# Local dilated attention gated by a SiLU feed-forward: the feed-forward of groups 2 and 3 by threes, one more attention chunk turned by DMA through spent key tiles

## The chip, the cores and the metric

One core of a Trainium2 chip runs the whole kernel. The metric is the device time of one execution in microseconds (us). Before the change it is 624.95 us, the median of three runs from 624.53 to 624.99 us.

## What is computed

The input is x with 2048 positions of 640 features, in float32. A layer norm of x feeds two branches, whose product is added to x:

```python
xn = _layernorm(x, axis=-1)
s = _A_ref(xn, A_wqkv, A_wo)          # attention, then a projection with wo
g = _silu(_B_ref(xn, B_w1, B_w2))     # silu(silu(xn @ w1) @ w2)
return x + s * g
```

The attention has 32 heads of 20 features. Each position looks at eight positions: its own and those 2, 4, ... 14 before it. w1 is 640 x 1536 and w2 is 1536 x 640.

## The kernel before, in words

**Tiles and groups.** The 2048 positions are cut into four groups of 512; the code counts them g = 0 to 3, and this text calls them group 1 to 4, as the change's title does. A group is a half of the sequence and a parity of its positions, so that the dilation of 2 becomes a dilation of 1 inside a group. In a group each of the 128 partitions holds T = 4 neighbouring positions. The 640 features are DC = 5 chunks of 128.

**Exact products out of rounded ones.** TensorE multiplies in the type float32r. To keep accuracy, every factor is split into a rounded high half and the rest (`th` and `tl` for data, `wh` and `wl` for weights, `sh` and `sl` inside the feed-forward), and each product is three matmuls: high by high, low by high, high by low.

**The stages.** For each group `qkv_phase` makes queries, keys and values in four quarters of 160 columns (`NQ = 4`), each quarter with 5 chunks x 4 tiles of positions x 3 matmuls into four of the six accumulator banks `acc`. ScalarE empties the banks (`evac_qkv`) into the tiles `Q[q]` and `KV[q]`. `KV[q]` holds K and V of one quarter with HALO = 7 earlier positions ahead of them; these come from the neighbour partition, so `halo` shifts 127 rows by one partition and 126 rows by two with DMAs. VectorE then does the attention of that quarter (`scores`, `values`) into the tile `O`. This runs long behind TensorE: VectorE finishes a group's attention while TensorE is in that group's feed-forward and the next group's quarters.

`ffn_phase` runs the feed-forward: `up(f)` makes one of FC = 12 chunks of the hidden layer (15 matmuls of 512 columns into a bank `rot`, then two SiLUs on ScalarE and a subtraction on VectorE), and `down(f)` multiplies that chunk by w2 into six `acc` banks. Within it lies `wo_phase`, the projection of the *previous* group's attention. For that, the previous group's `O` has to be turned (features on the partitions), chunk by chunk. There are two ways: `o_chunk` turns a chunk on TensorE (`split_t`, line 636: four transposes), and `turn_o` turns it by DMA (ScalarE copies the chunk into one tile, two DMA transposes carry it into a second tile, ScalarE joins it, VectorE makes the low half). The table `ON_DMA` says for each group which chunks go by DMA, and when.

**Weights.** 100 and more weight tiles pass through a ring of RING = 7 tiles `w0` to `w6`. At its first uses a weight is loaded raw (line 538) and split on the fly by ScalarE (line 573) and VectorE (line 577); at one of these uses the two halves are stored in DRAM (line 581, tiles `half_...`), and later uses load both halves at once with a DMA from the GpSimd queue (line 564), 640 KB each for a feed-forward chunk. A ring tile is loaded again when TensorE is done with it, and, where its halves are being stored, when that store has landed. The weights of the projection, wo, are split a second time and stored in group 3: `half_wo_0` to `half_wo_4`.

**What sets the order.** TensorE's order is the order in which the code records its operations (`plan(g)` for the feed-forward). All other engines get theirs from a list scheduler, `Weave`, that works with estimated durations and priorities; it orders the SP queue and the GpSimd queue too. An engine and a queue then run their list strictly in that order. In `halo`, each shift is cut at row 112, so it is issued as a DMA of 112 rows and one of 15 or 14 rows (line 751).

**What the steps of the prediction touch.** PE is TensorE, DVE is VectorE, ACT is ScalarE, POOL is GpSimd, SP is the queue that issues most DMAs. Line 636 is a transpose on TensorE, 751 a halo DMA, 581 a store of weight halves, 564 a load of them, 1130 to 1132 the matmuls of `up`, 1003 and 1005 those of `down` and of the projection, 956 to 958 those of the quarters, 1048 to 1051 the residual rows of a group (load, add on POOL, store).

Of the kernel before, what the change touches and what calls it, by code (L numbers as in the profile page):

```python
# [15 lines left out]
P = 128  # L16
S, D, F, H, DH = 2048, 640, 1536, 32, 20
# [4 lines left out]
CQ = HQ * DH  # L22
# [7 lines left out]
CA, CB = 384, 256  # L30
RING = 7
NS = 3
SINGLE = 6
RAW_AHEAD = 10
TURNS = 1
FIRST_AT = 44.0, 60.0
# [6 lines left out]
SUB_LATE = 3  # L43
ADD_LATE = 3
X_BY = {1: 2, 3: 0, 4: 1}
PACE0, PACE = -20.0, 12.0
WARM, WARM2 = 20, 3
HOLD = 3.4
# [11 lines left out]
BY_ACT = (0,)  # L60
IN_PARTS = 2
KEYS_FIRST = ((3, 0),)
QAT = 48
MORE = 32
OAT = 16
# [21 lines left out]
class Weave:  # L87
# [8 lines left out]
    LANES = 8  # L96
    RATE = 310e3
    LAND = 1.9
    QUICK = 4.0
    EARLY = 4.1, 3.9, 5.5, 5.2, 6.5, 7.3, 8.1, 8.85, 9.7  # L100
    TABLE = 1.28
    PATIENCE = 1.0
# [5 lines left out]
        self.writer, self.readers = {}, {}  # L108

    def add(self, eng, dur, fn, reads=(), writes=(), prio=0.0, lock=False, table=None, nbytes=0, more=0.0, late=0.0, at=0.0,  # L110
            spans=(), quick=False):
# [29 lines left out]
    def order(self):  # L141
# [21 lines left out]
        while len(done) < len(self.ops):  # L163
# [31 lines left out]
            free[e] = t + dur  # L195
            if o.nbytes:
                dma = max(dma, t + dur) + o.nbytes / self.RATE
                o.end = (self.EARLY[moved] if moved < len(self.EARLY) else t + dur + self.QUICK if o.quick else
                         dma + self.LAND + o.more)
# [99 lines left out]
def local_attention_silu_ffn(ctx: ExitStack, tc: tile.TileContext, x, wqkv, wo, w1, w2, out):  # L299
# [9 lines left out]
    xg = x.rearrange("b (g p j) d -> (b g) p j d", p=P, j=J)  # L309
    og = out.rearrange("b (g p j) d -> (b g) p j d", p=P, j=J)  # L310
    OL_AT = {10: 2}
    groups = [(h, par) for h in range(2) for par in range(2)]
    NG = len(groups)

    def rows(view, g):
        h, par = groups[g]
        return view[h, :, par::2, :]
# [71 lines left out]
    def free_for(old, new):  # L389

        add("DVE", 0.0, lambda: None, [], list(old) + list(new), 0)
# [2 lines left out]
        add("PE", dur, fn, reads, writes, spans=spans)  # L394
        clock[0] += dur

    def dma(fn, reads, writes, nbytes, prio, dur=0.45, more=0.0, quick=False):
        add("SP", dur, fn, reads, writes, prio, nbytes=nbytes, more=more, quick=quick)

    clock = [0.0]  # L400

# [12 lines left out]
    def plan(g):  # L414

        last = g == NG - 1
        todo = [("w1", 0)] + [("wo", 0)] * (g > 0)
        down = 0  # L420
        f = 1
        while f < FC:
            k = f // 2
            pair = f + 1 < FC and not (last and f > SINGLE)
            if g < TURNS and 1 <= k <= DC and k - 1 not in X_DMA:
                todo.append(("x", k - 1))
            if last and f in OL_AT:
                todo.append(("o", OL_AT[f]))
            if last and f == FC - 1:
                todo.append(("rest", (0, 1)))  # L430
            n = 2 if pair else 1
            todo += [("w1", u) for u in range(f, f + n)]
            f += n
            todo += [("w2", u) for u in range(down, down + n)]
            down += n
        return todo + [("w2", u) for u in range(down, FC)]

# [274 lines left out]
    def turn_o(g, c, i, out, into, at=0.0):  # L712

        qs = range(c * P // CQ, ((c + 1) * P - 1) // CQ + 1)
        keys = [("o", q, t) for q in qs for t in (0, 2)]
        xp = [(piece(XIN, k), ("xp", k)) for k in range(DC)]
        by, to = ((xp[0], xp[1]), (xp[2], xp[3]), (xp[4], (TURN, ("turn",))), (xp[1], xp[3]), (xp[0], xp[2]))[c]
        if g < NG - 1:
            by, to = ((TURN, ("turn",)), (SF, ("sf",))) if c % 2 == 0 else (xp[3], xp[4])
        if out:  # L720
            send(O, c, keys, "o", by, to, at)
        if into:
            join(to, by[0].rearrange("p (t n) -> p t n", t=T), both(by[1]), [], i, c, OH[i][:, c, :], OL[i][:, c, :], at)


    def q_keys(q, t):
        return [("q", q, t)] + [("q", q, t, k) for k in range(q if q == NQ - 1 else 0)]
# [14 lines left out]
    def halo(g, q):  # L742
        h, par = groups[g]
        kv = KV[q]
        own = kv[:, :, HALO:, :]
        kown = [(k, q, t) for k in ("kv", "own", "val") for t in range(T)]

        def shift(by, dst, src, tag, s=slice(0, 2), also=()):
            cut = 112
            for a, b in ((0, cut), (cut, P - by)):  # L750
                dma(lambda a=a, b=b: nc.sync.dma_start(kv[a + by:b + by, s, dst], own[a:b, s, src]),
                    kown, [("halo", q, tag, a, *also)], (b - a) * (s.stop - s.start) * CQ * 4 * (dst.stop - dst.start), clock[0],
                    quick=(g, q) in KEYS_FIRST)
# [174 lines left out]
    def qkv_phase(g, i, io):  # L928
# [7 lines left out]
            free_for([("xin", t) for t in range(T)], XP)  # L936
        if g in ON_DMA and g < NG - 1:
            free_for(["sf"], [("sf", 0), ("sf", 1)])
            free_for([("xin", 2), ("xin", 3)], XP[6:])
        for q in range(NQ):  # L940
            if g == 0 and q == 0:
                ps = first_quarter(i)
# [31 lines left out]
        turn_now(g, NQ, io)  # L974
        if g in ON_DMA and g < NG - 1:
            free_for([("sf", 0), ("sf", 1)], ["sf"])
            free_for(XP[6:], [("xin", 2), ("xin", 3)])

    def turn_now(g, q, io):
        for step in ON_DMA[g][0].get(q, ()) if g in ON_DMA else ():  # L980
            k, into, at = step
# [37 lines left out]
    TM = mm(CA) + mm(CB)  # L1019

    def wo_phase(g, i):
        banks = tm_banks()
        a, b = banks
        for c in range(DC):
            wh, wl, kh, kl = w_next("wo", c)
# [11 lines left out]
        if g == NG - 2:  # L1037
            for t in range(T):
                xr, kx = (XR[t], [("xr", t)]) if t < 3 else (PRV[:, :D], PRK)
                rest.append((t, xr, kx))  # L1040
                if t < 3:
                    dma(lambda t=t, xr=xr: nc.sync.dma_start(xr, rows(xg, g)[:, t, :]), [], kx, P * D * 4, clock[0] + 5)
            return
        add("DVE", HOLD, lambda: None, [("g", t, CA) for t in range(T)], ["hold"], 0)
        for t in range(T):
            s = take("xr", 3)
            xr = XR[s]
            dma(lambda t=t, xr=xr: nc.sync.dma_start(xr, rows(xg, g)[:, t, :]), [], [("xr", s)], P * D * 4, clock[0] + 5)
            add("POOL", po(D), lambda t=t, xr=xr: nc.gpsimd.tensor_tensor(out=xr, in0=xr, in1=G[:, t, :], op=OP.add),
                [("g", t, 0), ("g", t, CA)], [("xr", s)], 500, lock=True)  # L1050
            dma(lambda t=t, xr=xr: nc.sync.dma_start(rows(og, g)[:, t, :], xr), [("xr", s)], [], P * D * 4, clock[0] + 20)

    rest = []

# [205 lines left out]
```

## Time and profile before

| what | value |
|---|---|
| median of three runs | 624.95 us (624.53 to 624.99) |
| the profiled execution, its own time | 624.74 us |
| span of its instructions | 623.0 us |
| TensorE busy | 617.8 us, 99% of the span |
| VectorE busy | 541.4 us, 87% |
| ScalarE busy | 267.7 us, 43% |
| GpSimd busy | 114.9 us, 18% |
| DMA moved | 166.86 MB, mean 268 GB/s |
| TensorE clock granted | 1.0 |

Times in the views are in us from the span's start. A row of the timeline gives start, duration, engine, line, operation and its tiles (out<-in, buffer numbers left out), and in brackets how long the engine had been idle and what ended that. Matmuls overlap in the pipeline, so the *distance of their starts* is what one costs, not the duration shown. The stages of TensorE follow each other without a gap: the quarters of group 2 start at 144.81, those of group 3 at 297.0, those of group 4 at 448.8, and each group's feed-forward fills the time to the next.

### The profile page before, as it was taken

How to read it: one execution, taken by the hardware profiler on the slowest of the kernel's cores; microseconds unless marked ns; L12 is line 12 of the kernel's file. 1: busy time of each engine (PE TensorE's matmuls, PEld its weight loads, DVE VectorE, ACT ScalarE, POOL GpSimd, SP SyncE). 2: the span in 40 equal slices, each digit the busy share in tenths (PEclk: the TensorE clock that was granted, in tenths of full speed). 3: DMA queues.
4: the chain of work that ended last, by engine and by line, in shares of the span. 5: the costliest groups of instructions: out<-in, count | busy, mean ns of one | idle time of the engine just before them, and what ended most of it. 6: DMA issues, size and time to landing. Idle time of an engine off the chain costs nothing.

```text
span 623.0 us, 9035 instructions
## 1 busy us (share of the span) xinstructions
PE 617.8 (99%) x3403; PEld 558.4 (90%) x3403; DVE 541.4 (87%) x545; ACT 267.7 (43%) x493; POOL 114.9 (18%) x165
## 2 busy tenths in 40 slices
PE   9999999999999999999999999999999999999997
PEld 7888999998889989999888999999988999999997
DVE  7599899999788999899949999989937999898834
ACT  5445555364545224563543604174644353252220
POOL 4800000001110142111221115112222211111100
PEclk9999999999999999999999999999999999999999
DMA  9999999599999989975999999999699999688652
GB/s 296 310 309 318 331 387 375 195 325 267 297 285 317 322 241 319 234 231 139 227 270 258 351 341 304 162 245 355 171 235 270 286 332 269 197 235 246 184 190 86
DMA packets 102873, 166.86 MB, mean 268 GB/s; under 512 B 34365, under 2 KB 64541, under 8 KB 102829
## 3 DMA queue, kind: packets, MB, share of 16 engines
q1 hardware_dynamic: 76333, 86.56, 52.1%
q0 software_dynamic: 25952, 79.31, 45.3%
q8 instruction: 27, 0.44, 0.3%
q10 hardware_dynamic: 544, 0.41, 0.2%
q14 instruction: 17, 0.14, 0.1%
HBM read 107.91 MB, written 34.16 MB: 228 GB/s over the span
## 4 chain that ended last, share of the span: by engine, by line
PE 98%; DMA 0%; DVE 0%; issue 0%
PE acc L1003 22%; PE acc L1005 15%; PE acc L956 10%; PE acc L958 10%; PE acc L957 10%; PE rot L1131 9%; PE rot L1132 9%; PE rot L1130 9%; PE acc L893 2%; PE rot L636 1%; DMA xin<-in_A_x_dram 0%; PE rot L877 0%; PE rot L1116 0%; DVE st L862 0%; PE rot L836 0%; DVE gate L1084 0%
## 5 line engine op out<-in xcount | busy, mean ns | idle before, releaser
L1003 PE MATMUL acc<-w,sh 128*128 128x384 f32 x384 | 113.2, 334 | 0.0
L956 PE MATMUL acc<-w,th 128*128 128x512 f32 (+2 forms) x300 | 113.0, 377 | 0.0
L958 PE MATMUL acc<-w,th 128*128 128x512 f32 (+2 forms) x300 | 112.9, 376 | 0.0
L957 PE MATMUL acc<-w,tl 128*128 128x512 f32 (+2 forms) x300 | 112.8, 376 | 0.0
L776 DVE TENSOR_TENSOR pr<-q,kv 128x2560 f32<-128x2560 f32 x32 | 90.3, 2821 | 22.8 <-DMA kv<-kv 22.6
L1005 PE MATMUL acc<-w,sh 128*128 128x256 f32 x384 | 107.1, 279 | 0.0
L1143 ACT ACTIVATE sh<-rot 128x512 fp32r<-128x512 f32 x48 | 28.8, 599 | 155.4 <-PE rot L1132 155.3
L1130 PE MATMUL rot<-th,w 128*128 128x512 f32 x240 | 94.4, 393 | 0.0
L1132 PE MATMUL rot<-th,w 128*128 128x512 f32 x240 | 93.9, 391 | 0.0
L1131 PE MATMUL rot<-tl,w 128*128 128x512 f32 x240 | 93.8, 391 | 0.0
L810 DVE TENSOR_TENSOR pr<-q,kv 128x2560 f32<-128x2560 f32 x32 | 91.9, 2871 | 0.8
L779 DVE TENSOR_REDUCE l<-pr 128x128 f32<-128x2560 f32 x32 | 89.9, 2810 | 0.2
L564 POOL DMA_DIRECT2D w<-half_q x52 | 37.4, 719 | 234.5 <-DVE pr L815 97.1
L564 POOL DMA_DIRECT2D w<-half_w x72 | 38.9, 541 | 201.7 <-PE acc L1005 86.4
L815 DVE TENSOR_TENSOR pr<-pr 128x1280 f32<-128x1280 f32 x64 | 74.0, 1155 | 1.2
L1005 PEld LDWEIGHTS acc<-w,sh 128*128 128x128 f32 x384 | 72.2, 188 | 1.0
L1003 PEld LDWEIGHTS acc<-w,sh 128*128 128x128 f32 x384 | 72.1, 188 | 1.0
L958 PEld LDWEIGHTS acc<-w,th 128*128 128x128 f32 x300 | 56.3, 188 | 8.8
L956 PEld LDWEIGHTS acc<-w,th 128*128 128x128 f32 x300 | 56.3, 188 | 8.7
L957 PEld LDWEIGHTS acc<-w,tl 128*128 128x128 f32 x300 | 56.3, 188 | 8.7
L733 ACT ACTIVATE kv<-acc 128x320 f32<-128x320 f32 x64 | 28.0, 440 | 75.9 <-PE acc L958 74.5
L1003 PE MATMUL acc<-w,sl 128*128 128x384 f32 x192 | 57.8, 332 | 0.0
(115 smaller groups left out, 1040.3 us busy)
## 6 DMA issues: line engine op xcount, KB each, us to landing
w<-half_w POOLq DMA_DIRECT2D x72, 640.0 KB, 7.3
w<-half_q POOLq DMA_DIRECT2D x39, 512.0 KB, 5.1
half_w<-w SPq DMA_DIRECT2D x24, 640.0 KB
kv<-kv SPq DMA_DIRECT2D x15, 560.0 KB
w<-half_wo POOLq DMA_DIRECT2D x10, 640.0 KB, 6.9
kv<-kv SPq DMA_DIRECT2D x15, 420.0 KB
gate<-in_B_w_dram SPq DMA_DIRECT2D x16, 320.0 KB
w<-half_q POOLq DMA_DIRECT2D x13, 384.0 KB, 7.4
```

Of the source, the lines that this page charges most:

```text
L564: add("POOL", 1.0, lambda: nc.gpsimd.dma_start(both, src), [("half", u), ("half", u, "more")], [kh, kl], due + 10, nbytes=2 * n * P * 4)
L776: dve(2560, lambda t=t: nc.vector.tensor_tensor(out=PR, in0=win(qq[:, t:t + 2, :], W, 0), in1=win(kv[:, 0, t:t + 2, :], W, CQ), op=OP.mult ...
L779: dve(2560, lambda t=t: nc.vector.tensor_reduce(out=l[:, t:t + 2].rearrange("p t w h -> p (t w h)"), in_=PR.rearrange("p t w (h d) -> p (t ...
L810: dve(2560, lambda t=t, v=v: nc.vector.tensor_tensor(out=PR.rearrange("p t w (h d) -> p t (w h) d", d=DH), in0=e[:, t:t + 2].rearrange("p ...
L956: nc.tensor.matmul(o, hi, wh, start=c == 0, stop=False)
L957: nc.tensor.matmul(o, lo, wh, start=False, stop=False)
L958: nc.tensor.matmul(o, hi, wl, start=False, stop=c == DC - 1)
L1003: nc.tensor.matmul(a[t][0][:, :CA], st, w[:, :CA], start=first, stop=last)
L1005: nc.tensor.matmul(b[t // 2][0][:, h * CB:(h + 1) * CB], st, w[:, CA:], start=first and h == 0, stop=last, skip_group_check=True)
L1130: nc.tensor.matmul(h, wh[:, cs], TH[i][:, c, :], start=c == 0, stop=False)
L1131: nc.tensor.matmul(h, wh[:, cs], TL[i][:, c, :], start=False, stop=False)
L1132: nc.tensor.matmul(h, wl[:, cs], TH[i][:, c, :], start=False, stop=c == DC - 1)
```

## The change

- The feed-forward's order is now a table, `STEPS`. Groups 1 and 4 keep theirs (mostly pairs of `up`, then a pair of `down` that lags by one). Groups 2 and 3 go by threes: three `up`, then the same three `down`. In group 2 the projection now comes ahead of the first `up`; in group 3 it stays behind it.
- `wo_phase` gives the six banks to its tiles in another order.
- Of group 2's attention, chunk 3 is now turned by DMA too, so `qkv_phase` of group 3 turns chunks 0 to 3 by DMA and only chunk 4 on TensorE. Chunks 1, 2, 3 go through the K and V halves of `KV[1]`, `KV[2]`, `KV[3]` (`LENT`, `spare`, `lend`), whose old contents are spent and which are handed back before the new quarter is written; before, chunk 1 went through the tile `xin`.
- The residual rows of group 3 (`rest`, in `wo_phase`) may be loaded no earlier than their place in TensorE's order (`at=clock[0]`).
- The halo of group 3's last quarter isn't cut any more (`UNCUT`): one DMA of 127 rows and one of 126 rows in place of four.
- The scheduler's estimate of a DMA's latency is a number per DMA (`KEYS_IN`, `OUT_IN`) in place of one constant; with `OUT_IN` the stores of result rows no longer take one of the scheduler's eight lanes.

```diff
+LENT = None, 1, 2, 3, None
+KEYS_IN = 4.0
+OUT_IN = 6.0
+UNCUT = ((2,3),)
...
+    STEPS = [
...
+        (((0, 1, 2), (0, 1, 2)), ((3, 4, 5), (3, 4, 5)), ((6, 7, 8), (6, 7, 8)), ((9, 10, 11), (9, 10, 11))),
+        (((0,), ()), ((1, 2), (0, 1, 2)), ((3, 4, 5), (3, 4, 5)), ((6, 7, 8), (6, 7, 8)), ((9, 10, 11), (9, 10, 11))),
...
-        if g < NG - 1:
-            by, to = ((TURN, ("turn",)), (SF, ("sf",))) if c % 2 == 0 else (xp[3], xp[4])
+        lent = LENT[c] if g < NG - 1 else None
+        if lent is not None:
+            by, to = spare(0, lent), spare(1, lent)
+        elif g < NG - 1:
+            by, to = (TURN, ("turn",)), (SF, ("sf",))
...
-            for a, b in ((0, cut), (cut, P - by)):
+            for a, b in ((0, P - by),) if (g, q) in UNCUT else ((0, cut), (cut, P - by)):
...
-              NG - 2: ({0: ((0, 0, 4.0), (1, 0, 4.0)), 1: ((0, 1, 8.0), (1, 1, 8.0), (2, 0, 4.0)), 2: ((2, 1, 8.0),)},
-                       {(2, 4): (3,), (3, 4): (4,)}),
+              NG - 2: ({0: ((0, 0, 4.0), (1, 0, 4.0)), 1: ((0, 1, 8.0), (1, 1, 8.0), (2, 0, 0.0), (3, 0, 10.0)), 2: ((2, 1, 4.0),), 3: ((3, 1, 0.0),)},
+                       {(3, 4): (4,)}),
...
-        banks = tm_banks()
+        n = [bank() for t in range(T + T // 2)]
+        banks = [n[1], n[2], n[3], n[5]], [n[0], n[4]]
...
-                    dma(lambda t=t, xr=xr: nc.sync.dma_start(xr, rows(xg, g)[:, t, :]), [], kx, P * D * 4, clock[0] + 5)
+                    dma(lambda t=t, xr=xr: nc.sync.dma_start(xr, rows(xg, g)[:, t, :]), [], kx, P * D * 4, clock[0] + 5, at=clock[0])
```

What the scheduler makes of it on the SP queue: group 3's last halo (`kv3<-kv3`) stands in the same place, ahead of the store of the fourth wo chunk, but as two DMAs. First before, then after the change; `xr` are rows of x or raw weights, `half_wo` are stores of weight halves.

```order
L581 DMA half_wo_2_169<-w4_79 128x1280
L1048 DMA xr2_109<-in_A_x_dram 128x640
L751 DMA kv3_96<-kv3_96 112x2x640
L751 DMA kv3_96<-kv3_96 15x2x640
L751 DMA kv3_96<-kv3_96 112x2x480
L751 DMA kv3_96<-kv3_96 14x2x480
L581 DMA half_wo_3_170<-w5_80 128x1280
```

After the change the same stretch of the SP queue reads:

```order
L586 DMA half_wo_2_169<-w4_79 128x1280
L1059 DMA xr2_109<-in_A_x_dram 128x640
L764 DMA kv3_96<-kv3_96 127x2x640
L764 DMA kv3_96<-kv3_96 126x2x480
L586 DMA half_wo_3_170<-w5_80 128x1280
```

Only the form of the halo has moved; the store out of ring tile `w5` comes next in both.

On the GpSimd queue the loads after the projection follow the new order of the feed-forward. Before, with `half_w1_3` the weights of `up(3)` and `half_w2_2` those of `down(2)`:

```order
L564 DMA w3_78<-half_w2_1_139 128x1280
L564 DMA w4_79<-half_w1_3_140 128x1280
L564 DMA w5_80<-half_w1_4_141 128x1280
L1049 TENSOR_TENSOR xr2_109<-xr2_109,gate_106 128x640
L564 DMA w0_75<-half_w2_3_143 128x1280
```

After the change the same stretch is:

```order
L569 DMA w3_78<-half_w2_1_139 128x1280
L569 DMA w4_79<-half_w2_2_142 128x1280
L569 DMA w5_80<-half_w1_3_140 128x1280
L569 DMA w0_75<-half_w1_5_144 128x1280
L1060 TENSOR_TENSOR xr2_109<-xr2_109,gate_106 128x640
L569 DMA w6_81<-half_w1_4_141 128x1280
```

Ring tile `w5` now receives the weights of `up(3)`, before those of `up(4)`; every load behind it waits for it.

More of the change, by code (lines that the diff above doesn't have):

```diff
@@ L32 @@
 NS = 3
-SINGLE = 6
 RAW_AHEAD = 10
@@ L98 @@
     LAND = 1.9
-    QUICK = 4.0
     EARLY = 4.1, 3.9, 5.5, 5.2, 6.5, 7.3, 8.1, 8.85, 9.7
@@ L110, in add @@
     def add(self, eng, dur, fn, reads=(), writes=(), prio=0.0, lock=False, table=None, nbytes=0, more=0.0, late=0.0, at=0.0,
-            spans=(), quick=False):
+            spans=(), quick=0.0):
         o = Op()
@@ L197, in order @@
                 dma = max(dma, t + dur) + o.nbytes / self.RATE
-                o.end = (self.EARLY[moved] if moved < len(self.EARLY) else t + dur + self.QUICK if o.quick else
+                o.end = (self.EARLY[moved] if moved < len(self.EARLY) else t + dur + o.quick if o.quick else
                          dma + self.LAND + o.more)
@@ L311, in local_attention_silu_ffn @@
     OL_AT = {10: 2}
+    STEPS = [
[4 rows of a table added]
+    ]
     groups = [(h, par) for h in range(2) for par in range(2)]
@@ L395, in pe, with dma @@
         clock[0] += dur
-    def dma(fn, reads, writes, nbytes, prio, dur=0.45, more=0.0, quick=False):
-        add("SP", dur, fn, reads, writes, prio, nbytes=nbytes, more=more, quick=quick)
+    def dma(fn, reads, writes, nbytes, prio, dur=0.45, more=0.0, quick=0.0, at=0.0):
+        add("SP", dur, fn, reads, writes, prio, nbytes=nbytes, more=more, quick=quick, at=at)
     clock = [0.0]
@@ L418, in plan @@
         last = g == NG - 1
[L419 to L424, printed above, removed]
+        todo = [("wo", 0)] * (g > 0 and len(STEPS[g][0][1]) > 0)
+        k = 0
+        for ups, downs in STEPS[g]:
             if g < TURNS and 1 <= k <= DC and k - 1 not in X_DMA:
                 todo.append(("x", k - 1))
-            if last and f in OL_AT:
-                todo.append(("o", OL_AT[f]))
-            if last and f == FC - 1:
+            if last and ups[0] in OL_AT:
+                todo.append(("o", OL_AT[ups[0]]))
+            if last and ups[0] == FC - 1:
                 todo.append(("rest", (0, 1)))
[L431 to L436, printed above, removed]
+            todo += [("w1", f) for f in ups] + [("w2", f) for f in downs]
+            if not downs:
+                todo += [("wo", 0)] * (g > 0)
+            else:
+                k += 1
+        return todo
     units = []
@@ L717, in turn_o @@
         by, to = ((xp[0], xp[1]), (xp[2], xp[3]), (xp[4], (TURN, ("turn",))), (xp[1], xp[3]), (xp[0], xp[2]))[c]
-        if g < NG - 1:
-            by, to = ((TURN, ("turn",)), (SF, ("sf",))) if c % 2 == 0 else (xp[3], xp[4])
+        lent = LENT[c] if g < NG - 1 else None
[3 more added lines that the diff above has]
+            by, to = (TURN, ("turn",)), (SF, ("sf",))
+        if out and lent is not None:
+            for k in range(2):
+                lend(k, lent)
         if out:
@@ L723, in turn_o @@
             join(to, by[0].rearrange("p (t n) -> p t n", t=T), both(by[1]), [], i, c, OH[i][:, c, :], OL[i][:, c, :], at)
+        if into and lent is not None:
+            for k in range(2):
+                lend(k, lent, True)
     def q_keys(q, t):
@@ L749, in shift @@
             cut = 112
-            for a, b in ((0, cut), (cut, P - by)):
+            for a, b in ((0, P - by),) if (g, q) in UNCUT else ((0, cut), (cut, P - by)):
                 dma(lambda a=a, b=b: nc.sync.dma_start(kv[a + by:b + by, s, dst], own[a:b, s, src]),
-                    kown, [("halo", q, tag, a, *also)], (b - a) * (s.stop - s.start) * CQ * 4 * (dst.stop - dst.start), clock[0],
-                    quick=(g, q) in KEYS_FIRST)
+                    kown, [("halo", q, tag, k, *also) for k in (0, cut) if a <= k < b], (b - a) * (s.stop - s.start) * CQ * 4 * (dst.stop - dst.start), clock[0],
+                    quick=KEYS_IN * ((g, q) in KEYS_FIRST))
         for part in ((slice(0, 1),), (slice(1, 2), ["v"])) if (g, q) in KEYS_FIRST else ((),):
@@ L938, in qkv_phase @@
             free_for(["sf"], [("sf", 0), ("sf", 1)])
-            free_for([("xin", 2), ("xin", 3)], XP[6:])
         for q in range(NQ):
@@ L976, in qkv_phase @@
             free_for([("sf", 0), ("sf", 1)], ["sf"])
-            free_for(XP[6:], [("xin", 2), ("xin", 3)])
     def turn_now(g, q, io):
-        for step in ON_DMA[g][0].get(q, ()) if g in ON_DMA else ():
-            k, into, at = step
+        for k, into, at in ON_DMA[g][0].get(q, ()) if g in ON_DMA else ():
             turn_o(g, k, io, not into, into, clock[0] + at)
@@ L1050, in wo_phase @@
                 [("g", t, 0), ("g", t, CA)], [("xr", s)], 500, lock=True)
-            dma(lambda t=t, xr=xr: nc.sync.dma_start(rows(og, g)[:, t, :], xr), [("xr", s)], [], P * D * 4, clock[0] + 20)
+            dma(lambda t=t, xr=xr: nc.sync.dma_start(rows(og, g)[:, t, :], xr), [("xr", s)], [], P * D * 4, clock[0] + 20, quick=OUT_IN)
     rest = []
```

2 rows, old and new, of the table STEPS are left out of this document.

## The prediction

> **What bounds the kernel now.** I read the page first: engines, slices, the chain of waits.
>
> ```profile
> span 623.0 us, 9035 instructions
> PE 617.8 (99%) x3403; PEld 558.4 (90%) x3403; DVE 541.4 (87%) x545; ACT 267.7 (43%) x493; POOL 114.9 (18%) x165
> PEclk9999999999999999999999999999999999999999
> PE 98%; DMA 0%; DVE 0%; issue 0%
> ```
>
> TensorE is busy for 617.8 of 623.0 us at the full granted clock, and the chain that ended last is TensorE for 98%. The list of waits, asked for PE alone, has a single row:
>
> ```profile
> PE rot L849 <- POOL ident masks.py:199: 1.4, 1, 1.4
> ```
>
> So TensorE waits only at the start. The other 4 us are the last multiplications and the last store. Two things follow. The change can gain only what it takes out of TensorE's own work. And any lateness that reaches TensorE is paid in full, because behind it there is no idle time in which to catch up. The question is which waits were just hidden.
>
> Three more views tell where cover was thin. VectorE (timeline, the ends of the attention of groups 2 and 3):
>
> ```profile
> 315.22 0.49 DVE L818 TENSOR_TENSOR o<-pr 128x320 f32<-128x320 f32 x1
> 324.65 2.83 DVE L776 TENSOR_TENSOR pr<-q,kv 128x2560 f32<-128x2560 f32 x1 [8.34 <-DMA kv<-kv]
> 457.54 0.49 DVE L818 TENSOR_TENSOR o<-pr 128x320 f32<-128x320 f32 x1
> 471.64 2.83 DVE L776 TENSOR_TENSOR pr<-q,kv 128x2560 f32<-128x2560 f32 x1 [13.61 <-DMA kv<-kv]
> ```
>
> VectorE has 8.3 us in hand at group 3's start and 13.6 us at group 4's. The SP queue and the GpSimd queue just after group 3's quarters:
>
> ```profile
> 350.89 4.24 SPq L751 DMA_DIRECT2D kv<-kv  x4
> 359.86 0.33 SPq L581 DMA_DIRECT2D half_wo<-w  x1
> ```
>
> ```profile
> 363.36 0.53 POOL L564 DMA_DIRECT2D w<-half_w  x1 [2.91 <-DVE l L779]
> 373.25 0.53 POOL L564 DMA_DIRECT2D w<-half_w  x1 [9.36 <-DMA kv<-carry]
> 373.80 1.59 POOL L1049 TENSOR_TENSOR xr<-xr,gate 128x640 f32<-128x640 f32 x1
> ```
>
> The load at 373.25 is the one into ring tile w5. It is held back for 9.4 us by a DMA. The view names a small carry that was issued at 371.96, but the load doesn't touch that tile; by the code it has to wait for the store out of w5 (issued at 359.86), whose last step in the trace's semaphore events is at 372.7. That store stands in the SP queue right behind the four halo DMAs of 350.89. The queue's transfers finish in the order of their issue, so the halo sets when the store lands, and the store sets when the weights come. That costs nothing before the change: w5 gets the weights of up(4) then.
>
> **The change, part by part.** The sum goes against the profiled execution's own 624.74 us (span 623.0 and 1.74 around it), which lies 0.21 under the median of 624.95; I forecast on its scale. About 0.2% (1.25 us) is what a measurement of this kernel can tell from no change.
>
> *One chunk less on TensorE.* The chain in order of time has the turn that goes:
>
> ```profile
> 337.97 0.44 PE rot L636 x4
> ```
>
> Four transposes, 0.44 us of a path without slack: -0.44. All matmuls stay, their number and shapes too; the order by threes costs TensorE nothing by itself.
>
> *What replaces it.* Chunk 3 goes over ScalarE, SP and VectorE. Such a turn is one copy, one join and one rounding on ScalarE, 1.1 + 1.4 + 0.6 us, and one subtraction of 0.7 us on VectorE (the rows of 311.40 and 312.82 below are the join and the rounding; the copy's 1.1 us is an estimate that lies under the join of the same 128 x 512 values, and the subtraction is this row):
>
> ```profile
> 315.63 0.68 DVE L686 TENSOR_TENSOR tl<-turn,th 128x512 fp32r<-128x512 f32 x1
> ```
>
> The engines have room, but the tiles are the K and V halves of KV[1] to KV[3]: the quarter's banks can be emptied into them only after the join. The thinnest place is the end of group 3's second quarter:
>
> ```profile
> 311.40 1.38 ACT L681 ACTIVATE turn<-sf 128x1024 uint16<-128x1024 uint16 x1
> 312.82 0.63 ACT L685 ACTIVATE th<-turn 128x512 fp32r<-128x512 f32 x1
> ...
> 322.37 0.44 ACT L733 ACTIVATE kv<-acc 128x320 f32<-128x320 f32 x1 [8.92 <-PE acc L958]
> ...
> 324.41 0.44 ACT L733 ACTIVATE kv<-acc 128x320 f32<-128x320 f32 x1
> ```
>
> ```profile
> 325.57 0.39 PE L956 MATMUL acc<-w,th 128*128 128x512 f32 x1
> ```
>
> TensorE takes the first bank again at 325.57 (that matmul opens the third tile of the next quarter). In the new ScalarE order the eight query copies come first, then the four K/V copies, so the first bank is free at about 324.8 + 0.44 = 325.2: 0.3 us to spare. For that, ScalarE has to have sent chunk 3 and joined chunk 1 (1.1 + 1.4 + 0.6 = 3.1 us) by 322.4, so VectorE's last O has to be there by 319.3; it was at 315.7. I take nothing, and keep 0 to 3 us for it. VectorE's scores of that group start later, behind two subtractions that wait for ScalarE until about 329 instead of 324.65; with further work moved behind them I count some 9 us of lateness at the end of the group's attention. The 13.6 us at group 4's start hold that.
>
> *Projection first, in group 2.* In before, up(0) covers the split of the wo weights:
>
> ```profile
> 199.14 0.82 DVE L577 TENSOR_TENSOR w<-xr,w 128x640 fp32r<-128x640 f32 x1
> 201.41 2.18 DVE L626 TENSOR_SCALAR xin<-xin,mv,sd 128x640 f32<-128x640 f32 x4
> 205.40 1.56 DVE L577 TENSOR_TENSOR w<-xr,w 128x640 fp32r<-128x640 f32 x2 [0.87 <-ACT w L573]
> ```
>
> Now the projection starts some 3.4 us sooner and needs the third chunk's low half about 204.6. VectorE's new order has it right behind the four L626 rows, and the two short steps that stood ahead of them (1.0 us) behind it: 202.6 + 0.8 = 203.4. Cover 1.2 us; if it fails, at most the 2.8 us to the 206.2 of before. I take nothing. The new bank order takes the two free banks first, so no bank is waited for.
>
> *By threes, later residual rows.* A ring load has six tiles of work as cover in both orders; fewer loads of rows in the feed-forward of group 3 relieve the queue there. Nothing, and no gain, since no wait of TensorE is there to remove.
>
> *The uncut halo.* This is the term that decides. Before, a halo is 112 rows and 15 (or 14):
>
> ```profile
> q1 hardware_dynamic: 386, 1.44, 82.5%
> kv<-kv SPq DMA_DIRECT2D x1, 560.0 KB
> kv<-kv SPq DMA_DIRECT2D x1, 75.0 KB
> ```
>
> These rows are the DMA view of 350.8 to 355.2. No DMA of 127 rows is in the trace, so its cost is bounded from both sides. One end: it spreads over the 16 DMA engines as the 112 rows do, then it costs nothing and saves two issues. The other end: it goes to one engine. The trace's semaphore events bear on this. Of the 16 steps by which a DMA counts, a 112-row halo has all 16 at its landing; one of 15 rows has 15 there and one right at the issue; one of 14 rows has 14 and one jump at the issue; a carry of two rows has two. So the number of engines goes by a divisor of the rows: 16, 15, 14, 2. 127 is a prime, and 126 gives 14. I take one engine for the 127 rows. The Trainium skill's page "DMA: Bandwidth & Descriptors", section "Why a DMA increments its semaphore by 16 and not by 1", states it outright: of a DMA issued from SP, as many engines work as the largest number up to 16 that divides the slowest dimension, and it names 127 partitions as going to one. The semaphore counts of this trace agree for 112, 15, 14 and 2; no row here shows 127. By that page the sum is the forecast; by the 112-row row as the nearest it would be 624.3.
>
> The price: 127 rows are 254 runs of 2,560 B; the engine had 14 of them from the 112 rows and up to 2 from the 15. It gets 238 more, 609 KB. In the view above the queue moves 1.44 MB in 0.825 x 16 x 4.4 us = 58 us of engine time, 24.8 GB/s for one engine: 24.6 us. By the page's rows for the whole span,
>
> ```profile
> q1 hardware_dynamic: 76333, 86.56, 52.1%
> ...
> w<-half_w POOLq DMA_DIRECT2D x72, 640.0 KB, 7.3
> ```
>
> it is 86.56 MB in 0.521 x 16 x 623 us, 16.7 GB/s: 36.5 us. I take the fast end, because once the GpSimd queue stands still the engine has the halo almost alone. The store out of w5 has a sixteenth of its bytes on that engine, behind the halo, so the load into w5 is issued at 373.25 + 24.6 = 397.9. The DMA view of 373.2 to 373.9 has what this very load took to land:
>
> ```profile
> w<-half_w POOLq DMA_DIRECT2D x1, 640.0 KB, 4.3
> ```
>
> Against a median of 7.3 I take this 4.3, since the rest of the queue is as empty then: 402.2.
>
> ```profile
> 369.94 0.23 PE rot L1130
> ...
> 383.68 0.23 PE rot L1130
> ```
>
> These rows of the chain mark where up(1) and up(3) begin in before (by TensorE's own timeline the matmuls start 0.15 us earlier, 369.8 and 383.5), so two up and two down are 13.75 us and one step is 3.44. After, up(1), up(2) and three down come first: 369.8 - 0.44 + 13.75 + 3.44 = 386.5. The load into w5 now carries the weights of up(3). TensorE stands from 386.5 to 402.2: **+15.7 us**. The loads behind it (w0, then an addition of 1.6 us, then w6 for up(4) at 401.1, landed 405.5) arrive before up(4) at 405.6. Nothing gives the time back.
>
> Sum: 624.74 - 0.44 + 15.7 = **640.0 us**. Bounds of its own: the slow rate and the 7.3 us landing give 36.5 + 7.3 in place of 24.6 + 4.3, 14.9 more: 655. If the halo's engine is one of those that were done first (the store's landing events spread from 368.5 to 372.7), and a bit of overlap comes to it, 7 less: 633.
>
> **The rivals.** *The cover holds* (same, 0.35): the halo spreads over many engines, or the store doesn't wait for it; then only the transposes are left, 624.74 - 0.44 = 624.3. For it speaks that this halo isn't read before VectorE's scores of the last quarter, some 50 us later, and that TensorE had no wait at all. Against it the 9.4 us in which the GpSimd queue stood for this store already. It decides if the store lands before about 381.5 (386.5 less 4.3 and the issue). *The lent tiles come back late* (slower, 0.05): VectorE's last O of group 2 later than 319.3, then each us more keeps ScalarE from the banks and TensorE stands from 325.6 on; with 3 us, 624.3 + 2.7 = 627.0. The 3.6 us of slack speak against it. *Faster by over 1.25 us* (0.03) has no mechanism that I see: 0.44 us is all that leaves TensorE's path. Forecast: 0.57.
>
> **How the numbers follow.** Slower is the forecast and the late tiles, 0.57 + 0.05 = 0.62; same 0.35; faster 0.03. The likeliest case has the range 633 to 655. As the cover case alone holds more than 0.2, the range has to reach down to it: 624.0 (624.3 with the spread of the runs) to 655.
>
> **What would show it.** Right: a wait of TensorE near 386 at an L1130 successor for a load of w, the load into w5 issued near 398, and that store landing just ahead of it; the total PE busy lower by 0.4. Wrong: TensorE's list of waits still with one row, the load into w5 at 367 to 375; then the halo isn't slow, and the time is 624.3. A wait at 325 to 327 on ScalarE's L733 successor would show the second rival.

## The result, and the profile after

The changed kernel takes 641.58 us (median of six runs, 639.33 to 648.71), the kernel before 624.90 us beside it (624.53 to 625.14). The ratio is 1.0291, with a 95% interval from 1.0262 to 1.032: slower by 16 to 20 us (the medians lie 16.7 us apart). Here and in the experiments a ratio leaves out executions that were slow as a whole, so it isn't always that of the two medians. The profiled execution took 642.76 us, span 641.0. The page of after, the lines that answer to those of before:

```profile
span 641.0 us, 9035 instructions
...
PE 619.8 (97%) x3399; PEld 559.9 (87%) x3399; DVE 535.7 (84%) x545; ACT 271.5 (42%) x496; POOL 115.0 (18%) x165
...
PEclk9999999999999999999999996899999999999999
...
PE 85%; DMA 8%; DVE 3%; SPq 2%; ACT 1%; issue 1%; DVEq 0%; POOLq 0%; ACTq 0%
```

Four transposes are gone from TensorE, yet it is busy for 2.0 us longer; the chain that ended last now runs over DMAs for 8% of the span; and two slices of the granted clock are no longer 9. The list of TensorE's waits (line in the new numbering, what it waited for, us in total, times, longest):

```profile
PE rot L1141 <- DMA w<-half_w: 12.6, 1, 12.6
PE acc L968 <- ACT gate L1230: 3.1, 1, 3.1
PE rot L862 <- POOL ident masks.py:199: 1.4, 1, 1.4
PE rot L890 <- DVE xin L880: 0.5, 1, 0.5
```

The last two lie in the first 6 us and change nothing: group 2's quarters start at 144.66 in after and at 144.65 in before (by TensorE's own timeline; the 144.81 given above is a row of the chain, which starts some 0.15 us later). The first is the wait for the load into w5. Here is the SP queue (line 764 is the halo, 586 the stores of the wo halves), then the GpSimd queue (569 is a load of weight halves):

```profile
351.36 28.27 SPq L764 DMA_DIRECT2D kv<-kv  x2
379.83 2.05 SPq L586 DMA_DIRECT2D half_wo<-w  x1
```

```profile
363.44 0.53 POOL L569 DMA_DIRECT2D w<-half_w  x1 [2.91 <-PE acc L1015]
394.42 1.05 POOL L569 DMA_DIRECT2D w<-half_w  x2 [30.44 <-DMA half_wo<-w]
```

Two DMAs occupy the SP queue for 28.3 us (four took 4.2 us before). The store out of w5 is issued at 379.8 in place of 359.9, it lands at 393.9, and the load into w5 goes out at 394.4 in place of 373.25. In the semaphore events the 127-row DMA has one jump right at its issue and a single step at 390.9, so 15 of its 16 steps came at once. What moves meanwhile is told by the DMA view of 370 to 379 (first all packets, then the queue of SP: packets, MB, busy share of the 16 engines):

```profile
DMA packets 91, 0.25 MB, mean 27 GB/s; under 512 B 1, under 2 KB 1, under 8 KB 90
...
q1 hardware_dynamic: 88, 0.23, 6.3%
```

In this stretch the core's 16 DMA engines together move 27 GB/s, nearly all of it the halo (0.23 MB on SP's queue, which has nothing else under way). 6.3% of 16 engines is 1.0 engine: one engine carries the 127 rows, without a pause, and the others stand nearly still. TensorE's timeline where the weights arrive, and its granted clock in two stretches (the number ahead of the DMA share, which is the last but one):

```profile
399.80 0.80 PE L1141 MATMUL rot<-th,w 128*128 128x512 f32 x1 [12.59 <-DMA w<-half_w]
400.39 0.63 PE L1142 MATMUL rot<-tl,w 128*128 128x512 f32 x1
400.82 0.63 PE L1143 MATMUL rot<-th,w 128*128 128x512 f32 x1
...
404.41 0.39 PE L1143 MATMUL rot<-th,w 128*128 128x512 f32 x1
404.64 0.39 PE L1141 MATMUL rot<-th,w 128*128 128x512 f32 x1
```

```profile
399.80:404.00 4.20, 4.20 (x10) 3.33 (x11) 0.00 (x0) 0.92 (x1) 2.93 (x4) 0.50 1.08 402
404.00:408.00 4.00, 4.00 (x19) 3.30 (x18) 1.35 (x2) 1.09 (x2) 0.53 (x1) 0.99 1.08 403
```

After the 12.6 us of idling the starts of the matmuls are 0.43 us apart for 4.2 us, then 0.23 again; the granted clock is 0.50 and then 0.99. That is another 2.1 us.

The second wait, 3.1 us ahead of group 4's quarters, is read from the chain in order of time (start, us, what):

```profile
441.44 5.02 SPq L677
...
446.51 3.81 SPq L677
...
451.82 12.56 DMA gate<-gate
...
464.47 1.35 ACT xin L686
...
466.38 0.48 ACT gate L1230
...
466.91 0.51 PE acc L968
```

The chunks of group 3's attention that go by DMA transposes (line 677) were issued late. ScalarE stands in its order ahead of a join (line 686) until a transpose lands; the emptying of TensorE's banks (line 1230) is queued behind that join. In before the joins out of the tile `gate` were over at 437, 12 us ahead of the quarters.

By stage: TensorE reaches group 3's quarters 0.55 us later than before (297.51 against 296.96), their end 0.11 us later, group 4's quarters 18.09 us later, its own end 18.16 us later. So all but 0.1 us of it lies in group 3's feed-forward.

### The profile page after: what moved, and what is told of

It is laid out like the page before. It is cut to its first block, busy times and chain, and to the rows that moved or that the text cites. A ratio compares the mean times of both kernels' runs of the same rounds, so it can differ in the third digit from the quotient of the medians.

```text
span 641.0 us, 9035 instructions
## 1 busy us (share of the span) xinstructions
PE 619.8 (97%) x3399; PEld 559.9 (87%) x3399; DVE 535.7 (84%) x545; ACT 271.5 (42%) x496; POOL 115.0 (18%) x165
## 4 chain that ended last, share of the span: by engine, by line
PE 85%; DMA 8%; DVE 3%; SPq 2%; ACT 1%; issue 1%; DVEq 0%; POOLq 0%; ACTq 0%
PE acc L1013 18%; PE acc L1015 12%; PE acc L968 10%; PE acc L969 10%; PE acc L970 10%; PE rot L1141 7%; PE rot L1143 7%; PE rot L1142 7%; DMA gate<-gate 5%; DMA half_wo<-w 2%; PE acc L906 2%; SPq L677 2%; DMA w<-half_w 1%; PE rot L641 1%; DVE pr L828 0%
## 5 line engine op out<-in xcount | busy, mean ns | idle before, releaser
L1141 PE MATMUL rot<-th,w 128*128 128x512 f32 x240 | 95.3, 397 | 12.6 <-DMA w<-half_w 12.6
L968 PEld LDWEIGHTS acc<-w,th 128*128 128x128 f32 x300 | 56.3, 188 | 12.1 <-ACT gate L1230 3.4
L1141 PEld LDWEIGHTS rot<-th,w 128*128 128x128 f32 x240 | 45.6, 190 | 21.8 <-DMA w<-half_w 12.8
L1156 DVE TENSOR_TENSOR sl<-sf,sh 128x512 fp32r<-128x512 f32 x48 | 34.5, 719 | 34.8 <-ACT sf L1155 34.7
```

The costliest lines, as they stand in the source:

```text
L968: nc.tensor.matmul(o, hi, wh, start=c == 0, stop=False)
L1141: nc.tensor.matmul(h, wh[:, cs], TH[i][:, c, :], start=c == 0, stop=False)
```

## The experiments

Three theories stood at the start. Mine: 127 rows go to one DMA engine, this holds the SP queue, the store out of w5 and so the load behind it. Rival A: the order by threes or the lent tiles do the harm. Rival B: a DMA of more than 112 rows is slow as such, by its length. The times of the kernel before beside these runs are 624.99 to 625.0 us. In e1, e3 to e6, e8 and e10 all engines keep the changed kernel's order; in e7 and e9 the scheduler plans anew.

### e1: all orders kept, the halo cut again

```diff
+        parts = lambda a, b, by: ((0, 112), (112, b)) if b - a > 112 else ((a, b),)
...
-                dma(lambda a=a, b=b: nc.sync.dma_start(kv[a + by:b + by, s, dst], own[a:b, s, src]),
+                dma(lambda a=a, b=b: [nc.sync.dma_start(kv[c + by:d + by, s, dst], own[c:d, s, src]) for c, d in parts(a, b, by)],
```

> The changed kernel with every order kept, only the two uncut halo DMAs issued as four again (112 and 15 rows, 112 and 14). Theory (one engine has the 127 rows and holds the SP queue): the load into w5 is issued near 373 again, the wait of 12.6 us, the slow matmuls behind it (2.0 us) and the later wait of 3.1 us all go; 624.95 - 0.44 = 624.5 us (624.0 to 625.2). Rival A (the order by threes asks for w5's weights too early, or the lent tiles come back late): a wait of TensorE of several us stays near 387 or 325, 628 us or more.

Measured: 625.61 us, ratio 1.0005 (0.9987 to 1.0022). TensorE's list of waits is one row again, and the SP queue is held for 3.8 us:

```profile
PE rot L863 <- POOL ident masks.py:199: 1.4, 1, 1.4
```

```profile
351.96 3.81 SPq L765 DMA_DIRECT2D kv<-kv  x4
```

The whole loss goes with the form of two DMAs; rival A falls. But the time is 1.1 us above the 624.5 that I gave. Two pieces of that are followed up in e7 and e9.

### e2: the kernel before, with only this halo uncut

```diff
-            for a, b in ((0, cut), (cut, P - by)):
+            for a, b in ((0, P - by),) if (g, q) == (2, 3) else ((0, cut), (cut, P - by)):
```

All other rows of all engines are as in the kernel before.

> The kernel before with only group 3's last halo uncut (127 and 126 rows); five steps of TensorE stand ahead of the first user of w5 there too. Theory: the store out of w5 is issued some 27 us late, TensorE waits about 12.5 us for an L564 load near 387, runs some 4 us at half pace and perhaps waits once more (0 to 3 us): 624.9 + 14.5 to 17.5 = 639.4 to 642.4 us. Rival A (the threes are needed for the harm): 624.9 us, no wait.

Measured: 641.16 us (639.25 to 644.57), ratio 1.0267 (1.0234 to 1.0299). The SP queue, and the first row of TensorE's waits:

```profile
351.08 29.46 SPq L751 DMA_DIRECT2D kv<-kv  x2
```

```profile
PE rot L1130 <- DMA w<-half_w: 12.1, 1, 12.1
```

Neither the threes nor the lent tiles nor the projection's place is needed for the harm: here the first user of w5 is up(4), and it too is due near 387.

### e3 and e4: only the 127-row DMA, only the 126-row DMA uncut

```diff
+        parts = lambda a, b, by: ((0, 112), (112, b)) if b - a == 126 else ((a, b),)
```

> The changed kernel, every order kept, with only the 127-row DMA uncut; the 126 rows go as 112 and 14. Theory (127 is a prime, so one engine): as the change, 638 to 645 us, the next DMA of the SP queue is issued some 27 us late. Rival B (one DMA of over 112 rows is slow as such, each of the two gives its share by bytes, 635 and 473 KB): 624.5 + 17 x 0.57 = 634 us.

```diff
+        parts = lambda a, b, by: ((0, 112), (112, b)) if b - a == 127 else ((a, b),)
```

> The changed kernel, every order kept, with only the 126-row DMA uncut; the 127 rows go as 112 and 15. Theory (126 has the divisor 14, so 14 engines): no wait, 624.5 us (624.0 to 625.2). Rival B (share by bytes): 624.5 + 17 x 0.43 = 632 us.

Measured: e3 640.18 us (637.88 to 648.18), ratio 1.0233 (1.0217 to 1.0249); e4 625.73 us (625.51 to 626.35), ratio 1.0014 (1.0005 to 1.0024). The halo on the SP queue in e3, then in e4, three DMAs in each:

```profile
351.60 30.49 SPq L765 DMA_DIRECT2D kv<-kv  x3
```

```profile
351.63 2.94 SPq L765 DMA_DIRECT2D kv<-kv  x3
```

In e3 TensorE waits for 12.3 us, in e4 only at the start. The two DMAs carry 635 and 473 KB (of 1,024 bytes, as in the DMA view); a price by bytes would have been shared 57 to 43, and it is all with the 127 rows. Rival B is hurt: 126 rows are as long.

### e5 and e10: 126 + 1 rows, 113 + 14 rows

These two move the cut of the first DMA by a few rows, into three DMAs in e5 and, as before the change, four in e10.

```diff
+        parts = lambda a, b, by: ((0, 126), (126, b)) if b - a == 127 else ((a, b),)
```

> The changed kernel, every order kept, with the 127 rows as one DMA of 126 rows and one of a single row (the other DMA keeps its 126 rows): as many DMAs and the same bytes as a cut at 112, but each is over 112 rows long. Theory (the divisor counts, 126 gives 14 engines): no wait of TensorE, the SP queue isn't held, 625.6 us as with the cut halo (625.0 to 626.3). Rival B (a DMA of more than 112 rows is slow as such): 640 us.

```diff
+        parts = lambda a, b, by: ((0, 113), (113, b)) if b - a == 127 else ((0, 112), (112, b)) if b - a == 126 else ((a, b),)
```

> The changed kernel, every order kept, with the halo in four DMAs as before, but the larger part of the first cut at row 113 in place of 112 (113 and 14 rows; the other DMA 112 and 14). As many DMAs as with the cut halo and only one row moved from one to the other. Theory (the divisors count: 113 is a prime, so one engine gets 226 runs of 2,560 B): the next DMA is issued some 23 us late, the store lands near 390, TensorE waits 9 to 12 us near 387: 634 to 645 us. Rival (the length counts, or the spread is by shares of rows): 625.6 us.

Measured: e5 625.52 us (625.31 to 626.1), ratio 0.9998 (0.9981 to 1.0014); e10 641.73 us (636.41 to 650.27), ratio 1.0237 (1.0202 to 1.0271). The SP queue in e5, then in e10, and TensorE's wait in e10:

```profile
351.25 2.52 SPq L765 DMA_DIRECT2D kv<-kv  x3
```

```profile
351.23 27.17 SPq L765 DMA_DIRECT2D kv<-kv  x4
```

```profile
PE rot L1142 <- DMA w<-half_w: 9.0, 1, 9.0
```

One row more than 112 costs as much as fifteen more. 113 and 127 are primes, 112 and 126 have the divisors 16 and 14. The semaphore events say the same: the 113 rows have one jump at their issue and one single step, at 387.5; the 126 rows (e5) have one jump at the issue and 14 steps later. Rival B falls.

### e6: the 127-row DMA on ScalarE's queue

```diff
-                dma(lambda a=a, b=b: nc.sync.dma_start(kv[a + by:b + by, s, dst], own[a:b, s, src]),
+                dma(lambda a=a, b=b, e=nc.scalar if b - a == 127 else nc.sync: e.dma_start(kv[a + by:b + by, s, dst], own[a:b, s, src]),
```

> The changed kernel, every order kept, with the 127-row DMA issued from ScalarE's queue in place of SP's; the 126 rows and the stores stay on SP. It tells the two ways apart in which the slow halo could delay the store out of w5. Queue (the SP queue's own order and its room hold the store): SP is free, the store is issued near 358 and shares only a sixteenth with the slow engine, it lands by 382, no wait at 387: 625.6 us, at most 628. Engine (whatever goes to that one DMA engine waits behind the 650 KB): the store lands near 390 again, wait of 10 to 12 us, 637 to 642 us.

Measured: 637.87 us (637.58 to 638.64), ratio 1.0195 (1.016 to 1.023). The time lies in the range of the second forecast (637 to 642), but neither forecast has the way it came about. The store out of w5 was free: issued at 357.5, landed at 369.6, and TensorE doesn't wait at 387. But the halo now shares its engine with the loads and the SP queue: in the DMA view its own queue moves 10 packets from 359 to 363, beside busy loads, and 36 from 411 to 415, when the loads have stopped. It lands only at 417.6, 65.9 us after its issue, and the loss comes back elsewhere. The waits of the SP queue, then those of ScalarE, then TensorE's:

```profile
SPq L1062 <- DMA kv<-kv: 41.1, 1, 41.1
```

```profile
ACT xin L686 <- DMA gate<-turn: 24.8, 2, 22.9
```

```profile
PE rot L1141 <- ACT sf L1155: 10.6, 1, 10.6
```

The kernel's DMAs count on eight semaphores in turn. The second of the result stores that SP begins at 376.2 is the eighth DMA after the halo and so has the halo's semaphore; it stood for 41.1 us until the halo had landed. The transposes behind it were late, ScalarE stood for 22.9 us ahead of a join, and TensorE for 10.6 us. So the queue's order explains the wait for w5, the engine explains how long the halo takes, and with another queue the wait only moves.

### e8: half of the 127-row DMA

```diff
+        parts = lambda a, b, by, s: ((0, 127, slice(0, 1)), (0, 112, slice(1, 2)), (112, 127, slice(1, 2))) if b - a == 127 else ((0, 112, s), (112, b, s)) if b - a == 126 else ((a, b, s),)
```

> The changed kernel, every order kept, with only the K half of the 127-row DMA uncut (127 rows of 2,560 B, 325 KB); the V half goes as 112 and 15 rows, the 126 rows as 112 and 14. Theory: one engine takes 325 KB at the 16.8 GB/s of the change's trace (650 KB in 38.8 us) in 19.4 us, so the halo lands near 372, the store near 375, the load into w5 near 380, and TensorE needs it at 387.2: the cover holds, 625.6 us (625.0 to 627). A price in proportion (rival: half the bytes, half the loss): 633 us.

Measured: 627.21 us (625.29 to 637.06 in ten runs), ratio 1.0024 (1.0004 to 1.0044). The SP queue, and what TensorE waits for:

```profile
351.41 18.01 SPq L765 DMA_DIRECT2D kv<-kv  x5
```

```profile
PE rot L1142 <- ACT sf L1156: 1.2, 1, 1.2
```

The half halo lands at 377.8, not at 372: 325 KB took 25.2 us, 12.9 GB/s. Until about 371 weight loads are under way, with 0.66 MB on the GpSimd queue from 364 to 368 and 0.04 MB from 368 to 372, and the engine has to serve those as well. The load into w5 is issued at 381.9 and lands at 386.5, 0.7 us ahead of 387.2. In the profiled execution the cover holds by a hair, as the theory has it and a proportional price (633) doesn't, though each step came some 6 us later than the theory said and the median lies 0.2 us above its range. The runs up to 637 were not profiled; whether the cover failed in them stays open.

### e7: the halo cut, up(0) ahead of the projection in group 2 too

```diff
-UNCUT = ((2,3),)
+UNCUT = ()
...
-        (((0, 1, 2), (0, 1, 2)), ((3, 4, 5), (3, 4, 5)), ((6, 7, 8), (6, 7, 8)), ((9, 10, 11), (9, 10, 11))),
+        (((0,), ()), ((1, 2), (0, 1, 2)), ((3, 4, 5), (3, 4, 5)), ((6, 7, 8), (6, 7, 8)), ((9, 10, 11), (9, 10, 11))),
```

> The changed kernel with the halo cut and with group 2's feed-forward in group 3's order, so that up(0) stands ahead of the projection again; the plan is made anew. With the halo cut alone, group 2's projection ran 3.60 us a chunk against 3.44 in the kernel before and in groups 3 and 4. Theory (it is slow because it follows the four short transposes directly): the projection takes 17.2 us in place of 18.05 and the time is 625.6 - 0.7 = 624.9 us, at or just under the kernel before (624.0 to 625.3). Rival (the raw wo weights or the new order of the banks make it slow): 18.05 us again, 625.6 us.

Measured: 625.03 us, ratio 0.9998 (0.9978 to 1.0018). Fourteen us from within group 2's projection, in before (202 to 216), in after (200 to 214) and in e7 (202 to 216); behind PE's busy time stands its number of matmuls:

```profile
202.00:216.00 14.00, 14.00 (x100) 14.00 (x99) 13.10 (x12) 4.50 (x7) 2.12 (x4) 1.00 1.08 317
```

```profile
200.00:214.00 14.00, 14.00 (x95) 14.00 (x94) 13.67 (x14) 6.04 (x8) 2.95 (x5) 1.00 1.12 327
```

```profile
202.00:216.00 14.00, 14.00 (x100) 14.00 (x99) 13.06 (x12) 4.49 (x7) 2.12 (x4) 1.00 1.11 317
```

With the projection first, TensorE makes 95 matmuls in 14 us where it makes 100 otherwise, without a wait in the list and at the full clock: 18.05 us for the projection in place of 17.21. Behind up(0) it is 17.21 again, with the raw wo weights and the new bank order still there, so these two are not the reason. That it is the four short transposes right ahead of it fits, but no run puts them there alone. TensorE ends at 618.41, 0.85 us sooner than in before; the time is nevertheless that of before, and e9 asks why.

### e9: e7, with two DMAs fewer

```diff
-UNCUT = ()
+UNCUT = ((1, 3), (2, 3))
...
-            for a, b in ((0, P - by),) if (g, q) in UNCUT else ((0, cut), (cut, P - by)):
+            for a, b in ((0, P - by),) if (g, q) in UNCUT and by == 2 else ((0, cut), (cut, P - by)):
```

> The kernel of the last run with up(0) ahead of the projection and the halo cut, with the 126-row DMA of two halos uncut (last quarters of groups 2 and 3): two DMAs fewer on SP, so that the last store of the kernel counts on another semaphore, the last one that the closing checks come to, as in the kernel before. TensorE ended at 618.4 us there against 619.3 in the kernel before, but from the last landing to the end it took 1.8 us against 1.1. Theory (the place of the last store among the closing checks makes these 0.7 us): 625.0 - 0.7 = 624.3 us, 0.6 under the kernel before (624.0 to 624.7). Rival (the end varies by itself): 625.0 us.

Measured: 624.28 us, ratio 0.9998 (0.9982 to 1.0014). Nine of its twelve runs (624.05 to 624.56) lie under the lowest of the 17 runs of before beside it (624.77), but the interval of the ratio holds 1, so this is no shown gain. What the traces show of the end: SP checks the eight semaphores one after the other, and what comes behind the last store's own is still to be done. In e7 the last store counts on the second of the eight and lands at 621.06, the span ends 1.77 us later (e1: the same semaphore, 1.66 us); in e9 it counts on the last, lands at 621.36, and the span ends 1.06 us later, as in before (621.91 and 1.06). The six checks more take 0.42 us in e7, 0.06 to 0.1 us each; the other 0.3 us pass before a later step of SP's closing, and why is not shown. (TensorE ends 0.3 us later in e9 than in e7, so of the 0.7 us some 0.4 are left in the two profiled times.) Of the 1.1 us by which e1's median lies over the forecast, 0.54 us are group 2's feed-forward and 0.6 us this end. In e1's profiled execution, 0.3 us above its median, TensorE is also 0.6 us late by the end of group 1; this is not explained.

## Why the prediction was right, point by point

**The deciding step held.** The 127 rows went to one engine; the store out of w5, and the load behind it, came late; up(3) had to wait; nothing gave the time back. e3, e4, e5 and e10 show the divisor, e1 and e2 that no other part is needed. The Trainium skill's page "DMA: Bandwidth & Descriptors", section "Why a DMA increments its semaphore by 16 and not by 1", has this rule, and adds that the steps of the engines that aren't used are counted at the issue. The traces agree: 127 and 113 rows have a jump at the issue and one single step behind it, and the 127 rows keep 1.0 engine busy.

**The way had one part more.** I had the store queued behind the halo's data. In the trace already the issue of the next DMA, the 126 rows, was held: it ended at 379.6, 11.3 us before the halo landed (e10: 375.7 and 11.8; e8: 365.1 and 12.6). From there the store took another 14 us, and this part went as forecast: fifteen of its sixteen steps are there at 385.4, the last one only at 393.9, 2.9 us behind the halo (e8: 374.4, then 381.4, with the halo at 377.8). The order of landing that I leaned on held for these transfers (in before the four parts of the halo land at 367.1, 368.0, 371.2 and 371.4, the store at 372.7), but it is no rule of the queue: in before 15 of SP's 310 DMAs land ahead of the one issued just before them, nine of them small carries.

**The sizes.** The load was issued 21.2 us late (24.6 forecast), landed in 5.3 us (4.3), and TensorE stood from 387.2 to 399.8, 12.6 us, where I had 386.5 to 402.2, 15.7 us. The rate of one engine over the whole halo was between my two: 650,240 bytes in 38.4 us from 352.5 to 390.9 are 16.9 GB/s. But it is no single rate: from 370 to 379, with nothing else under way, 0.23 MB in 9 us are some 25 GB/s, and by difference only some 7 GB/s before 370, beside the loads (an estimate, if the 25 GB/s held to the end). So the fast end was the right choice for the reason given. That the 609 KB more delayed the load by 21.2 us and not by 24.6 is the overlap that the prediction allowed for in its lower bound; the traces don't say where it lies.

**Two terms were missing.** First, 2.1 us of half clock behind the wait. The Trainium skill's page "TensorE: Matmul & The Clock Gate", section "Part 1: The HAM clock gate (the "warmup" mystery)", says that after an idle window of about 3.4 us the array goes at half rate until it has been busy for as long. The runs agree in the main: waits of 9.0, 10.6, 12.3 and 12.6 us were each followed by some 4 us at half pace, 1.9 to 2.1 us lost, the wait of 12.1 us (e2) by 3.0 us, 1.5 us lost, and the waits of 1.2 and 3.1 us by none. Second, the wait of 3.1 us for ScalarE. I had looked at VectorE's 13.6 us at group 4's start for lateness. The 9 us that I counted there were right: in e1, where TensorE isn't held, VectorE ends group 3's attention 9.9 us later than before and has 4.0 us left. In after it ends 29.3 us later and still has 2.1 us left, because group 4's quarters start 18.1 us later too:

```profile
489.50 2.82 DVE L789 TENSOR_TENSOR pr<-q,kv 128x2560 f32<-128x2560 f32 x1 [2.12 <-DMA kv<-kv]
```

But I had not looked at ScalarE, which in its fixed order waits for late transposes ahead of the emptying of banks. The profiles of e2, e3 and e10 don't have this wait, so it isn't a fixed part of the price. The runs of after, e2, e3 and e10 spread by 5 to 14 us each; whether that is this wait in other sizes was not profiled and stays open.

**The small edits.** The chunk less is worth what was said: group 3's quarters take 51.43 us in place of 51.88. The lent tiles came back in time; ScalarE empties the banks from 325.23 (I had 324.8; TensorE doesn't wait there) and VectorE's scores start at 329.21 (I had 329):

```profile
325.23 1.44 ACT L746 ACTIVATE kv<-acc 128x320 f32<-128x320 f32 x4
```

```profile
329.21 2.82 DVE L789 TENSOR_TENSOR pr<-q,kv 128x2560 f32<-128x2560 f32 x1
```

"Projection first: I take nothing" was wrong by 0.85 us: no wait came, but a slower pace. The threes aren't quite nothing: group 2's feed-forward is 100.53 us in place of 99.99, so without the projection's 0.85 the rest of it gains 0.3; group 3's gains 0.14 in e1.

The sum: -0.45 (chunk) + 0.54 (group 2) - 0.14 (threes in group 3) + 12.6 + 2.1 + 3.1 = 17.75 of the 18.02 us between the two profiled executions. The forecast of +15.3 came near because the wait was put 3.1 us too long and 5.2 us of consequences were left out: the mechanism was right, but that the sum came so close is in part luck, two errors against each other. The range, 624.0 to 655, says little by itself, as it also took in the case without any wait. One of the signs named did not come: TensorE's busy time was to fall by 0.4 us and rose by 2.0, which is -0.45 + 0.54 - 0.14 + 2.1.

## What to carry to other kernels

Before you merge or cut a DMA, look at the divisors of its row count: 126 rows were as cheap as 112 here, 127 and 113 cost 13 to 17 us. The slow transfer's price was not paid by its own reader here but by what was queued behind it: follow the queue, the tile that the next transfer frees, and the in-order engine that stands for it. And when TensorE has to wait long, add the half clock behind the wait: 1.5 to 2.1 us behind waits of 9 us and more here, nothing behind 3.1 us; no run has a wait in between.

## What the runs showed of the hardware that was not expected

- One DMA on one engine holds the issue of the next DMA of its queue for 13 us (127 runs of 2,560 B, e8), 24 us (226 runs, e10) and 27 to 29 us (254 runs, e2, e3 and after), each time until some 11 to 13 us of its own work are left.
- The same DMA on another queue takes longer, 65.9 us against 39.6, and holds the SP queue by its semaphore, which the eighth next DMA shares (e6).
- A projection that follows four short transposes runs at 95 matmuls in 14 us, with 512-column matmuls ahead of it at 100, and it doesn't catch up in its 18 us (after and e1 against before and e7); that the transposes cause it isn't shown.
- Which of eight semaphores the last store counts on goes with 0.7 us at the end (1.7 to 1.8 us from the last landing in e1 and e7, 1.06 in before and e9).
